# Transposing the softmax of the landmark queries on VectorE and moving it by DMA, in a fused Nystrom attention and feed-forward kernel

## The chip, the cores and the metric

The kernel runs on one core of a Trainium2 chip. A core has a matrix engine (TensorE, PE in the profile; its weight loads have a row of their own, PEld), a vector engine (VectorE, DVE), a scalar engine (ScalarE, ACT), a general engine (GpSimd, POOL) and a queue engine that here only issues DMAs (SyncE, SP). DMAs are also issued from POOL's and ACT's queues. The engines run side by side, each through its own list of instructions in order, and wait for one another by semaphores.

The metric is the device time of one execution, in microseconds. Three runs of the kernel before took 279.04, 278.62 and 277.09 us; the median is 278.62.

## What is computed

The reference, cut to its core: Nystrom attention over 8 batches, 8 heads, 576 tokens of 64 features, with 32 landmarks, each the mean of 18 tokens, and behind it a multiplicative feed-forward layer.

```python
q_lm = q.reshape(B, H, 32, 18, D).mean(axis=3)      # landmarks
k_lm = k.reshape(B, H, 32, 18, D).mean(axis=3)
A  = softmax(scale * q    @ k_lm^T)                 # 576 x 32
Bm = softmax(scale * q_lm @ k_lm^T)                 # 32 x 32
C  = softmax(scale * q_lm @ k^T)                    # 32 x 576
Z  = Bm^T / (norm1(Bm) * norminf(Bm) + 1e-6)
for _ in range(6):
    Z = 2 * Z - Z @ Bm @ Z
x = A @ Z @ C @ v                                   # 4608 x 512 over all heads
out = ((x @ w1) * (x @ w2)) @ w3 @ w_out            # 4608 x 512
```

## The kernel before, in words

**Units of work.** A quad is four heads of one batch: 16 quads, n = 0 to 15, two to a batch b. With 32 landmarks a head, the landmarks of a quad fill the 128 partitions. w3 @ w_out is computed once at the start (tasks `w3n`, `wf`, `wt`, `mm`), so that each batch's dense part needs two products alone: d (x by w1 and w2, 192 tokens at a time) with the product of both on VectorE (f), and g (by w3 w_out, 128 tokens at a time), copied out by ScalarE (h) and stored on SP's queue (`st`).

**One quad.** Q and K are loaded from POOL's queue (`lq`), transposed on VectorE (`tk`, `tq`), summed to landmarks on POOL (`ma`, `mb`, lines 529 and 536), or for the first two quads on TensorE. `S{n}` multiplies the landmark queries by K into the PSUM tile `wide` (`psS`), of which there is one. VectorE takes the rows' maximum (`sm`, lines 585 and 586), copies the 32 columns of B's scores out (`bo`, line 593), ScalarE takes the exponential (`se`, line 599) into `ec`, the E of the title, 128 landmarks (four heads by 32) by 576 tokens. To multiply E by V, tokens must lie on partitions: TensorE transposes E back into `wide` in four pieces of 128 columns and one of 64 (task `T{n}`, lines 607 and 609), and ScalarE copies that to `ecT` (`cm` and `cr`, lines 614 and 619). Only then is `wide` free for the next quad's scores. `C{b}` multiplies E by V (tiles `vb`, loaded on SP's queue, line 504), in 80 small matmuls of 32 columns of weights for both quads. The A side (`A`, `am`, `as`, `ae`, `au`, `an`, `tA`, `aT`) goes by beside it.

**Groups.** The inverse is iterated for two batches together (`ba` to `Z`), on TensorE in 32x32 tiles, and joined to C by `W`; `U{b}` multiplies the result by w1 and w2, and the batch's dense part follows.

**What sets the order.** Class `Plan` holds a list scheduler that runs while the kernel is built. Each task has an engine, a duration, what it needs, which buffers it takes and gives back, and a priority; the planner runs through time with a model of the engines and of the DMA queues and writes one order, and each engine's instructions are issued in it. `T0` and `PER` (65 and 20) set when a batch's dense part is due, `att`, `lane` and `cvt` the due times of quads, groups and of C. On TensorE a task's mode (full array, or tiles of 128x32, 64x32, 32x32, 128x64) has a bonus if it is the last task's (`MP`, `MT`, `MY`), so that modes stay together. An engine never overtakes its own list: who waits holds up all that is behind.

The lines that matter for the change:

```python
    def c_trans(n):                                     # line 603
        ...
            for c in range(4):
                nc.tensor.transpose(out=psS[:, 0, 128 * c:128 * c + 128], in_=ec[:, 128 * c:128 * c + 128],
                                    identity=ident[:, :])
            nc.tensor.transpose(out=psS[0:64, 1, 128:256], in_=ec[:, 512:S], identity=ident[:, :])
...
    def cv_mm(b):                                       # line 770
        ...
                        mm(ps[r, 64 * qd:64 * qd + 64], ecTs[at(f"ecT{n}")][:, c, r],
                           vbs[at(f"vb{n}")][:, h, c, :], start=(c == 0), stop=(c == 4), pos=(0, 32 * h))
```

Of the kernel before, what the change touches and what calls it, by code (L numbers as in the profile page):

```python
# [15 lines left out]
S = 576  # L16
# [9 lines left out]
MT = 7.0  # L26
MY = 2.0
# [18 lines left out]
class Plan:  # L46
# [6 lines left out]
    SLACK = 0.05  # L53

# [40 lines left out]
    def _transfers(self, limit):  # L95


        while True:
# [3 lines left out]
            if act:  # L102
                all_ = sum(h[2].share for h in act)
                stop = min(stop, self.clock + min(h[1] * all_ / h[2].share for h in act))
                for h in act:
                    h[1] -= max(0.0, stop - self.clock) * h[2].share / all_
# [8 lines left out]
    def run(self):  # L115
# [4 lines left out]
        def ended(t, end):  # L120
# [8 lines left out]
            for u in after.get(t.name, ()):  # L129
                waiting[u.name] -= 1  # L130
                if not waiting[u.name]:
                    u.ready = max(self.by[d].end for d in u.deps)
                    avail[u.eng].append(u)
# [14 lines left out]
        while len(order) < n:  # L148
# [41 lines left out]
            if t.move:  # L190
                self.queues[e].append([at + (dur + 0.75 if e == "POOL" else min(dur, 0.45)), t.move, t])
            else:
                ended(t, at + dur + t.lat)
# [5 lines left out]
def kernel(  # L199
# [41 lines left out]
    P.ring("vb", NV)  # L241
    ecs = slots(fixed, 2, [128, S], FP32, "ec")
    ecTall = fixed.tile([128, 4, 5, 128], FP32, name="ecT")
# [41 lines left out]
    T0 = 65.0  # L285
# [5 lines left out]
    def att(n):  # L291
        bs = GROUPS[GOF[n // 2][0]]
        k = n - 2 * bs[0] - 2 * len(bs) + 4
        first = dense(bs[0]) - 55.0 + 7.5 * k
        return max(12.0 + 6.0 * n, first)
# [7 lines left out]

    NE = int(2.0)
# [23 lines left out]
    def const_e():  # L328
        nc.gpsimd.memset(vball[64:128, :, :, 4, :], 0.0)
        nc.gpsimd.memset(ecTall[64:128, :, 4, :], 0.0)  # L330
        nc.gpsimd.memset(lmTall.rearrange("p i a l e -> p (i a l e)").bitcast(FP32), 0.0)

# [10 lines left out]
    add("ce", "POOL", 2.4, const_e, deps=["cb"], prio=-4.0)  # L343
# [59 lines left out]

    def w3_hi(j, h, c0, c1):
        def fn():
            nc.scalar.activation(out=w3t[at(f"w3t{j}")][:, 0, 128 * c0:128 * c1], in_=w3_src(j, h, c0, c1),  # L406
# [3 lines left out]
    def w3_lo(j, h, c0, c1):  # L410
        def fn():
            c, t = slice(128 * c0, 128 * c1), w3t[at(f"w3t{j}")]
            nc.vector.scalar_tensor_tensor(out=t[:, 1, c], in0=w3_src(j, h, c0, c1), scalar=WSC,  # L413
                                           in1=t[:, 0, c], op0=ALU.mult, op1=ALU.subtract)
        return fn

    def w34_mm(j, c, part=None):
        def fn():
            ps = bank(at(f"pw{j}"))
            t = w3t[at(f"w3t{j}")]  # L420
            cc = slice(128 * c, 128 * c + 128)
            if part != 1:
                mm(ps, t[:, 0, cc], wo[:, 0, c, :], start=(c == 0), stop=False)
            if part != 0:
                mm(ps, t[:, 0, cc], wo[:, 1, c, :], start=False, stop=False)
                mm(ps, t[:, 1, cc], wo[:, 0, c, :], start=False, stop=(c == 7))
# [8 lines left out]
    W1 = 0.0  # L435
    JS = int(3.0)
    JH = 0.0
# [4 lines left out]
    def w34_tasks():  # L442
        for j in range(8):
            p0 = 4.0 + 7.7 * j
            add(f"w3n{j}", "SP", 0.43 if j < PEB else 1.7, load_w3(j), acq=[("w3n", f"w3n{j}", 1, 3 if j == 0 and PEB else 2)],
                prio=-0.01 if j == 0 else 0.1 + 0.01 * W1 - 0.005 if j == 1 else p0 - 10.0,
                after=0.0 if j < 2 else max(0.0, p0 - 10.0 - 4.0), move=1.42 if j < PEB else 1.8,
                lat=1.7, share=3.8 if j < PEB else 2.5)
            if j == 0:
                for c in range(8):  # L450
                    if c % 2 == 0:
                        add(f"wf{c}", "SP", 1.72, load_wout(c), prio=0.1 + 0.01 * c, move=1.55, lat=1.7, share=2.1)
# [9 lines left out]
            for h, (c0, c1) in enumerate(cuts):  # L462
# [7 lines left out]
                    acq=[] if h else [("w3t", f"w3t{j}", 1, 8)], rel=[f"ptr{j}{h}"], prio=p0 - 3.5 + h)  # L470
# [3 lines left out]
            for c in range(8):  # L474
                hi, lo = [f"woh{c}", f"wh{j}{part[c]}"], [f"wol{c}", f"wl{j}{part[c]}"]
                bank1 = [("P", f"pw{j}", 1, 1)] if c == 0 else []
                if j < JS:
# [3 lines left out]
                        rel=[f"w3t{j}"], prio=p0 + 0.7 * c, mode="full")  # L481
                    continue
                add(f"mm{j}{c}", "PE", 0.65, w34_mm(j, c), deps=hi + lo + ([f"mm{j}{c - 1}"] if c else []),
                    acq=bank1, rel=[f"w3t{j}"], prio=p0 + 0.7 * c, mode="full")
# [12 lines left out]
    def load_v(n):  # L497
        def fn():
            b, qd = divmod(n, 2)
            vb = vbs[at(f"vb{n}")]  # L500
# [81 lines left out]
    def s_max(n):  # L582
        def fn():
            mx = tinies[at(f"mx{n}")]
            nc.vector.reduce_max(out=mx[:, 0:1], in_=s_cols(), axis=AX.X)
            nc.vector.tensor_scalar(out=mx[:, 1:2], in0=mx[:, 0:1], scalar1=-SCALE, scalar2=None, op0=ALU.mult)  # L586
        return fn

    def b_out(n):
        def fn():  # L590
            b, qd = divmod(n, 2)
            g, i = GOF[b]
            nc.vector.tensor_copy(out=bscs[at(f"bsc{g}")][:, 2 * i + qd, :], in_=psS[:, 1, 64:96])
        return fn

    def s_exp(n):
        def fn():
            b, qd = divmod(n, 2)
            nc.scalar.activation(out=ecs[at(f"ec{n}")], in_=s_cols(), func=AXF.Exp,  # L599
                                 scale=SCALE, bias=tinies[at(f"mx{n}")][:, 1:2], accum_out=tinies[at(f"tc{b}")][:, 2 + qd:3 + qd])  # L600
# [11 lines left out]
    def c_main(n):  # L612
        def fn():
            nc.scalar.copy(out=ecTs[at(f"ecT{n}")][:, 0:4, :].rearrange("p c x -> p (c x)"), in_=psS[:, 0, :])
        return fn

    def c_rest(n):
        def fn():
            nc.scalar.copy(out=ecTs[at(f"ecT{n}")][0:64, 4, :], in_=psS[0:64, 1, 128:256])
# [87 lines left out]
    def quad_tasks(n):  # L707
# [4 lines left out]
            after=max(L0, p - (20.0 if n < 4 else 20.0)), move=3.3, lat=0.9, share=4.6)  # L712
        add(f"lv{n}", "SP", 1.72, load_v(n), acq=[("vb", f"vb{n}", 1, 1)], deps=["ce"] if n < 4 else [], prio=cvt(b) - 8.0 + qd, after=max(12.0, cvt(b) - 8.0 - 3.0 + 3 * qd), move=1.95, lat=1.8, share=1.1)
# [10 lines left out]
        else:  # L724
# [11 lines left out]
            acq=[("S", f"S{n}", 1, 3)], rel=[f"Tk{n}", f"lmT{n}"], prio=p, mode="full")  # L736
# [8 lines left out]
        add(f"sm{n}", "DVE", 0.83, s_max(n), deps=[f"S{n}"], acq=[("tiny", f"mx{n}", 1, 1)], prio=p)  # L745
        new = n == 2 * GROUPS[GOF[b][0]][0]
        add(f"bo{n}", "DVE", 0.1, b_out(n), deps=[f"S{n}"] + ([] if new else [f"bo{n - 1}"]),
# [440 lines left out]
```

## Time and profile before

| | |
|---|---|
| median of three runs | 278.62 us (277.09 to 279.04) |
| profiled execution, its own time | 278.43 us |
| its span, first to last instruction | 276.6 us |
| granted TensorE clock | 0.995 |
| busy PE / DVE / ACT / POOL | 259.1 / 185.2 / 194.7 / 121.5 us |
| DMA packets | 26732, 37.32 MB, mean 135 GB/s |

The span is 1.8 us shorter than the execution's time. The page cuts the span into 40 slices of 6.9 us, with the busy tenths of each engine in each:

```profile
PE   3997799989989999999999999999999999999992
DVE  2659989979649995975887957776764562542530
ACT  3666858357469789867997698599858647758741
POOL 9435787996958884918866811003010000000000
DMA  7999999999763552895937671112111121122123
```

In the first nine slices the loads fill the DMA engines (240 to 259 GB/s in the page's row of bytes). From the thirteenth slice on TensorE is busy 90% or more in all slices but the last. DVE, ACT and POOL do the attention side until about the thirtieth slice and then only feed the dense part. A group of lines gives busy time, the mean of one instruction, and the idle time ahead of it with what ended it. A matmul's own duration holds its way through the array, so its pace is read from starts that follow each other, not from its mean.

### The profile page before, as it was taken

Reading aid. Unit: us, or ns where it says so; the run is one execution under the profiler, and the core shown is the slowest. Engines: PE = TensorE matmul, PEld = TensorE weight load, DVE = VectorE, ACT = ScalarE, POOL = GpSimd, SP = SyncE. Lnnn points to the kernel's source line nnn. Section 1 sums busy time; section 2 is a strip of 40 time slices with the busy share of each in tenths; the row PEclk is TensorE's granted clock in tenths of the full one; section 3 lists DMA queues with packets and bytes.
Section 4 is the critical chain, followed back from the end, with each engine's and each line's share of the span. In section 5 each row is a group of like instructions: output and inputs, shape, how many; then the busy total and the mean of one; then the engine's idle time right before and its main releaser. Section 6 shows DMA issues by size and latency. Waiting matters only on the chain.

```text
span 276.6 us, 9700 instructions
## 1 busy us (share of the span) xinstructions
PE 259.1 (94%) x3908; PEld 171.4 (62%) x3908; DVE 185.2 (67%) x526; ACT 194.7 (70%) x551; POOL 121.5 (44%) x145
## 2 busy tenths in 40 slices
PE   3997799989989999999999999999999999999992
PEld 3663464645447776766578667766875765765761
DVE  2659989979649995975887957776764562542530
ACT  3666858357469789867997698599858647758741
POOL 9435787996958884918866811003010000000000
PEclk9999999999999999999999999999999999999998
DMA  7999999999763552895937671112111121122123
GB/s 245 252 254 255 259 243 256 240 252 216 128 105 69 89 97 100 227 220 121 180 79 192 168 207 40 38 47 72 41 40 40 57 61 59 58 78 76 40 77 115
DMA packets 26732, 37.32 MB, mean 135 GB/s; under 512 B 3264, under 2 KB 16832, under 8 KB 26688
## 3 DMA queue, kind: packets, MB, share of 16 engines
q1 hardware_dynamic: 19664, 24.91, 30.4%
q0 software_dynamic: 6784, 11.54, 24.4%
q8 instruction: 30, 0.49, 0.7%
q10 hardware_dynamic: 240, 0.26, 0.3%
q14 instruction: 14, 0.11, 0.1%
HBM read 38.80 MB, written 9.44 MB: 174 GB/s over the span
## 4 chain that ended last, share of the span: by engine, by line
PE 59%; DMA 16%; POOL 14%; DVE 4%; ACT 3%; issue 2%; SPq 0%; POOLq 0%; ACTq 0%
PE bank L276 53%; POOL ls L536 6%; DMA nat<-in_q_dram 6%; POOL ls L529 5%; DMA u<-in_moe_w_out_dram 4%; PE wide L276 3%; DMA nat<-in_k_dram 3%; DMA ecT<-in_moe_w_out_dram 2%; POOL ah L681 2%; DMA osb<-in_moe_w_dram 2%; PE wide L607 1%; DVE wo L371 1%; POOL nat L492 1%; PE bank L690 1%; ACT asb L1020 1%
## 5 line engine op out<-in xcount | busy, mean ns | idle before, releaser
L276 PEld LDWEIGHTS <-u 128*128 128x128 f16 x960 | 80.4, 98 | 32.5 <-issue 6.4
L1026 DVE TENSOR_TENSOR ab<-asb,bank 128x192 f16<-128x192 f16 x192 | 59.2, 346 | 43.2 <-ACT asb L1020 42.8
L276 PE MATMUL bank<-aT,u 128*128 128x192 f16 x768 | 77.0, 246 | 0.0
L276 PE MATMUL bank<-w,ab 128*128 128x512 f16 (+1 forms) x296 | 73.4, 374 | 0.0
L1020 ACT CAST asb<-bank 128x192 f16<-128x192 f32 x192 | 56.5, 333 | 22.3 <-PE bank L276 20.3
L276 PE MATMUL bank<-wo,u 128*128 128x512 f16 x192 | 47.8, 379 | 2.7 <-DVE wo L371 1.5
L529 POOL TENSOR_TENSOR ls<-nat 128x1152 f32<-128x1152 f16 x14 | 33.2, 2373 | 26.9 <-DMA nat<-in_q_dram 12.0
L536 POOL TENSOR_TENSOR ls<-ls 128x128 f32<-128x128 f32 (+2 forms) x56 | 40.7, 727 | 3.8
L276 PEld LDWEIGHTS <-ab 128*128 128x128 f16 x296 | 26.9, 98 | 20.8 <-issue 2.9
L681 POOL TENSOR_TENSOR ah<-ea,tiny 128x512 f16<-128x512 f32 (+1 forms) x16 | 18.5, 1159 | 44.0 <-DVE tiny L675 35.8
L938 ACT CAST u<-bank 128x512 f16<-128x512 f32 x64 | 34.4, 605 | 3.4 <-PE bank L276 3.4
L1052 ACT ACTIVATE osb<-bank 128x512 f32<-128x512 f32 x35 | 21.2, 605 | 8.8 <-PE bank L276 8.8
L566 ACT COPY lmT<-lmu 32x128 f16<-32x128 f16 x64 | 18.8, 294 | 4.6 <-DVE lmu L557 3.7
L276 PE MATMUL bank<-w,wT 64*32 64x512 f16 x512 | 18.9, 380 | 0.3 <-ACT u L938 0.2
L276 PEld LDWEIGHTS bank<-xz 32*32 32x32 f32 x768 | 11.2, 105 | 8.4 <-issue 2.1
L276 PE MATMUL bank<-xz 32*32 32x64 f32 (+1 forms) x768 | 14.8, 213 | 0.3 <-DVE xz L884 0.3
L599 ACT ACTIVATE ec<-wide,tiny 128x576 f32<-128x576 f32 x16 | 12.0, 749 | 4.4 <-DVE tiny L586 3.6
L413 DVE SCALAR_TENSOR_TENSOR u<-bank,u 128x512 f16<-128x512 f32 (+2 forms) x17 | 10.9, 638 | 5.6 <-ACT u L406 5.6
L276 PEld LDWEIGHTS <-Tq 128*128 128x128 f16 x160 | 10.6, 97 | 5.3 <-issue 1.9
L406 ACT ACTIVATE u<-bank 128x512 f16<-128x512 f32 (+2 forms) x17 | 9.7, 571 | 5.3 <-PE bank L276 4.5
L521 DVE STREAM_TRANSPOSE Tk<-nat 128x448 f32<-128x448 f32 (+1 forms) x32 | 13.1, 447 | 0.0
L674 DVE TENSOR_REDUCE tiny<-ea 128x16 f32<-128x512 f32 (+1 forms) x16 | 11.7, 732 | 1.4 <-ACT ea L668 1.4
(95 smaller groups left out, 322.5 us busy)
## 6 DMA issues: line engine op xcount, KB each, us to landing
vb<-in_v_dram SPq DMA_DIRECT2D x32, 160.0 KB, 4.3
out_dram<-osb SPq DMA_DIRECT2D x37, 128.0 KB, 2.3
nat<-in_k_dram POOLq DMA_DIRECT2D x16, 288.0 KB, 6.0
nat<-in_q_dram POOLq DMA_DIRECT2D x16, 288.0 KB, 7.8
vb<-in_v_dram SPq DMA_DIRECT2D x32, 128.0 KB, 4.4
out_dram<-osb SPq DMA_DIRECT2D x16, 256.0 KB, 2.4
w3n<-in_moe_w_dram SPq DMA_DIRECT2D x16, 128.0 KB, 7.7
w<-in_moe_w_dram POOLq DMA_DIRECT2D x8, 256.0 KB, 10.3
```

The costliest lines, as they stand in the source:

```text
L276: nc.tensor.matmul(out_, lhsT, rhs, start=start, stop=stop, **({} if pos is None else {"tile_position": pos}))
L521: nc.vector.transpose(out=T[:, to:to + r1 - r0].rearrange("p r l e -> p (r l e)").bitcast(FP32), in_=nats[at(f"nat{n}")][:, t, r0:r1].rear ...
L529: nc.gpsimd.tensor_tensor(out=l, in0=nat[:, :, 0:9, :], in1=nat[:, :, 9:18, :], op=ALU.add)
L536: nc.gpsimd.tensor_tensor(out=l[:, :, x:x + m, :], in0=l[:, :, x:x + m, :], in1=l[:, :, y:y + m, :], op=ALU.add)
L566: nc.scalar.copy(out=lm[r, :, h, :], in_=u[r].rearrange("p t l e -> p t (l e)"))
L599: nc.scalar.activation(out=ecs[at(f"ec{n}")], in_=s_cols(), func=AXF.Exp, scale=SCALE, bias=tinies[at(f"mx{n}")][:, 1:2], accum_out=tinies ...
L674: nc.vector.reduce_sum(out=t[:, 20:20 + g], in_=eas[at(f"ea{n}")][:, 0:g, :], axis=AX.X)
L681: nc.gpsimd.tensor_tensor(out=ahs[at(f"ah{n}")][:, 0:g, :], in0=eas[at(f"ea{n}")][:, 0:g, :], in1=tinies[at(f"ta{n}")][:, 0:g].unsqueeze(2 ...
L938: nc.scalar.copy(out=uu[at(f"u{b}{qd}")][:, wi, 512 * half:512 * half + 512], in_=bank(at(f"pU{b}{wi}{half}{qd}")))
L1020: nc.scalar.copy(out=asb[at(f"as{b}{j}{th}")], in_=bank(at(f"pD{b}{j}{th}"))[:, 0:THIRD])
L1026: nc.vector.tensor_mul(ab[:, j, c0:c0 + THIRD], asb[at(f"as{b}{j}{th}")], bank(at(f"pD{b}{j}{th}"))[:, THIRD:2 * THIRD])
L1052: nc.scalar.activation(out=osb[at(f"os{t}")], in_=bank(at(f"pE{t}")), func=AXF.Copy, scale=2.0 ** -12)
```

## The change

For quads 6 to 15 (batches 3 to 7; `NT` is 6) E isn't transposed on TensorE. VectorE transposes it in 32x32 blocks into `ecx` (`e_trans`, task `et`): afterwards tokens lie on partitions, but each block still stands on the 32 partitions of its head. 16 DMAs a batch on SP's queue (`e_move`, tasks `lx{b}{x}`, four to a task, one for each head) then move each block row from the 32 partitions of head h to the 32 partitions of token group x in `ecT`, for both quads at once, in runs of 640 or 512 bytes. `ecx` is their source, one buffer for a batch; `ecT` is laid out with the head ahead of the column group in all quads. `wide` is given back after the exponential and the copy of B's scores. The five transposes and both copies of these quads go.

For all quads the copy of B's scores (`bo`) and the factor on the maximum move from VectorE to ScalarE. The memset of `ecT` becomes a task of its own, behind the w_out work (`cz`). V's buffers are named by n modulo 4. The product of w3's fourth block is split into a high and a low part as the first three were (`JS` 4), the high part's priority moves forward (`JH` 3), the second w3 load goes behind the first w_out load (`W1`). Planner constants change: `T0` 65 to 64, `MT` 7 to 6, `MY` 2 to 2.5, latencies and shares of the loads, the due times of the w1/w2 loads, and a margin (`ROOM`) for tasks that are due early.

The diff's core:

```diff
-MT = 7.0
-MY = 2.0
+MT = 6.0
+MY = 2.5
...
-    ecTall = fixed.tile([128, 4, 5, 128], FP32, name="ecT")
+    ecTall = fixed.tile([128, 4, 4, 5, 32], FP32, name="ecT")
+    ecx = fixed.tile([128, 2, 4, 5, 32], FP32, name="ecx")
+    P.ring("ecx", 1)
...
-    T0 = 65.0
+    T0 = 64.0
...
+    NT = 2 * int(3.0)
...
-        nc.gpsimd.memset(ecTall[64:128, :, 4, :], 0.0)
...
+    def const_f():
+        nc.gpsimd.memset(ecTall[64:128, :, :, 4, :], 0.0)
...
+    add("cz", "POOL", 0.5, const_f, deps=[f"wol{c}" for c in range(4)], prio=1.5)
...
-    W1 = 0.0
-    JS = int(3.0)
-    JH = 0.0
+    W1 = 1.0
+    JS = int(4.0)
+    JH = 3.0
...
-            nc.vector.tensor_scalar(out=mx[:, 1:2], in0=mx[:, 0:1], scalar1=-SCALE, scalar2=None, op0=ALU.mult)
...
-            nc.vector.tensor_copy(out=bscs[at(f"bsc{g}")][:, 2 * i + qd, :], in_=psS[:, 1, 64:96])
+            nc.scalar.copy(out=bscs[at(f"bsc{g}")][:, 2 * i + qd, :], in_=psS[:, 1, 64:96])
...
+            nc.scalar.activation(out=mx[:, 1:2], in_=mx[:, 0:1], func=AXF.Copy, scale=-SCALE)
...
+    def e_trans(n):
+
+        def fn():
+            x, ec = ecx[:, n % 2], ecs[at(f"ec{n}")]
+            nc.vector.transpose(out=x[:, :, 0:4].rearrange("p x c l -> p c x l"),
+                                in_=ec[:, 0:512].rearrange("p (c x t) -> p c x t", c=4, x=4))
+            nc.vector.transpose(out=x[:, 0:2, 4], in_=ec[:, 512:S].rearrange("p (x t) -> p x t", x=2))
+        return fn
+
+    def e_move(b, x):
+        def fn():
+            i = P.slot[f"ecT{2 * b}"][0]
+            w = 5 if x < 2 else 4
+            for h in range(4):
+                nc.sync.dma_start(
+                    out=ecTall[32 * x:32 * x + 32, i:i + 2, h, 0:w, :].rearrange("p q c l -> p q (c l)"),
+                    in_=ecx[32 * h:32 * h + 32, :, x, 0:w, :].rearrange("p q c l -> p q (c l)"))
         return fn
...
-                add(f"lw{s}{qd}{wi}", "POOL", 0.62, load_w12(s, qd, wi), prio=T0 - 12.0 + 3.0 * s + wi,
-                    after=T0 - 12.0 - 4.0 + 3.0 * s, move=1.5, lat=0.9, share=2.1)
+                add(f"lw{s}{qd}{wi}", "POOL", 0.62, load_w12(s, qd, wi), prio=T0 - 10.0 + 5.0 * s + wi,
+                    after=T0 - 10.0 - 4.0 + 5.0 * s, move=1.4, lat=1.83, share=5.3)
...
-            acq=[("S", f"S{n}", 1, 3)], rel=[f"Tk{n}", f"lmT{n}"], prio=p, mode="full")
+            acq=[("S", f"S{n}", 1, 2 if n >= NT else 3)], rel=[f"Tk{n}", f"lmT{n}"], prio=p, mode="full")
...
-        add(f"T{n}", "PE", 0.54, c_trans(n), deps=[f"se{n}", "cb"], rel=[f"ec{n}"], prio=p + 2.0, mode="full")
-        add(f"cm{n}", "ACT", 0.5, c_main(n), deps=[f"T{n}"], acq=[("ecT", f"ecT{n}", 1, 1)], rel=[f"S{n}"],
-            prio=p + 2.5)
-        add(f"cr{n}", "ACT", 0.18, c_rest(n), deps=[f"T{n}", f"cm{n}"], rel=[f"S{n}"], prio=p + 2.5)
+        if n >= NT:
+            add(f"et{n}", "DVE", 0.8, e_trans(n), deps=[f"se{n}"], acq=[] if qd else [("ecx", f"ecx{b}", 1, 4)],
+                rel=[f"ec{n}"], prio=p + 2.0)
+            for x in range(4 * qd):
+                add(f"lx{b}{x}", "SP", 1.72, e_move(b, x), deps=[f"et{n - 1}", f"et{n}", "cz"],
+                    acq=[] if x else [("ecT", f"ecT{n - 1}", 2, 1)], rel=[f"ecx{b}"], prio=p + 3.0 + 0.1 * x,
+                    move=0.45, lat=1.9, share=0.8)
+        else:
+          add(f"T{n}", "PE", 0.54, c_trans(n), deps=[f"se{n}", "cb"], rel=[f"ec{n}"], prio=p + 2.0, mode="full")
+          add(f"cm{n}", "ACT", 0.5, c_main(n), deps=[f"T{n}", "cz"], acq=[("ecT", f"ecT{n}", 1, 1)], rel=[f"S{n}"],
+              prio=p + 2.5)
+          add(f"cr{n}", "ACT", 0.18, c_rest(n), deps=[f"T{n}", f"cm{n}"], rel=[f"S{n}"], prio=p + 2.5)
```

## The prediction

> **What bounds the kernel now.** I read the shares of the engines first, then the busy time by stage, then the timeline of TensorE, then the waits.
>
> ```profile
> PE 259.1 (94%) x3908; PEld 171.4 (62%) x3908; DVE 185.2 (67%) x526; ACT 194.7 (70%) x551; POOL 121.5 (44%) x145
> ```
> ```profile
> 20.00:78.00 58.00, 52.51 (x681) 28.39 (x680) 50.13 (x121) 35.02 (x92) 46.55 (x52) 1.00 1.02 223
> 78.00:100.00 22.00, 20.36 (x370) 15.46 (x369) 18.88 (x51) 18.95 (x60) 16.88 (x20) 1.00 0.48 84
> 100.00:207.00 107.00, 106.53 (x1794) 74.19 (x1792) 78.96 (x241) 85.35 (x257) 46.21 (x47) 1.00 0.48 121
> 207.00:271.40 64.40, 64.33 (x867) 42.64 (x864) 27.75 (x89) 43.52 (x122) 0.00 (x0) 1.00 0.19 63
> ```
> Columns of the stages: from and to, length, then busy PE, PE's weight loads, DVE, ACT, POOL (instructions in brackets), granted clock, DMA share, GB/s. From 100 us to the end of the matmuls PE rests 0.5 us in 171. Is busy also dense? In the timeline of the last stage, four and sixteen matmuls follow each other without a hole:
>
> ```profile
> 255.06 1.81 PE L276 MATMUL bank<-aT,u 128*128 128x192 f16 x20
> 256.70 1.03 PE L276 MATMUL bank<-w,ab 128*128 128x512 f16 x4
> ```
> Twenty matmuls of 192 columns take 256.70 - 255.06 = 1.64 us, 82 ns each, and this pace is the same wherever no wait is printed. So work taken off PE after 78 us comes off the span, until another engine is late.
>
> **A. The transposes of E on PE (line 607, 609), taken from quads 6 to 15.**
>
> ```profile
> 88.59 0.61 PE L607 MATMUL wide<-ident,ec 128*128 128x128 f32 x4
> 89.03 0.27 PE L609 MATMUL wide<-ident,ec 128*64 128x128 f32 x1
> 89.14 1.81 PE L276 MATMUL bank<-aT,u 128*128 128x192 f16 x20
> ```
> From 88.59 to the start of the next work at 89.14 is 0.55 us a quad; ten quads give **-5.5 us**. All ten stand after 88 us, in the dense stages.
>
> A rule of the Trainium skill speaks against this part: VectorE: DVE Perf Modes, sections "The three transpose paths" and "Rules for kernel authors", sends a 128x128 transpose to TensorE where its result may go to PSUM, and gives 390 ns there against 311 ns on VectorE, which turns 32x32 blocks alone. With its 390 ns for each of five transposes, an estimate, part A would be -19.5 us; the row's 0.55 us for five pipelined ones decides, and the sum goes by it.
>
> **B. What comes with it on ACT and DVE.**
>
> ```profile
> L614 ACT COPY ecT<-wide 128x512 f32<-128x512 f32 x16 | 9.7, 606 | 0.7 <-PE wide L609 0.6
> L619 ACT COPY ecT<-wide 64x128 f32<-64x128 f32 x16 | 4.3, 270 | 0.0
> L400 DVE STREAM_TRANSPOSE bank<-w3n 128x512 f32<-128x512 f32 x8 | 5.6, 705 | 0.0
> L521 DVE STREAM_TRANSPOSE Tq<-nat 128x64 f32<-128x64 f32 x8 | 1.6, 202 | 0.0
> L586 DVE TENSOR_SCALAR tiny<-tiny 128x1 f32<-128x1 f32 x16 | 2.5, 154 | 0.6
> L593 DVE COPY bsc<-wide 128x32 f32<-128x32 f32 x16 | 3.0, 187 | 3.8 <-ACT ec L599 3.6
> ```
> ACT loses 10 x (0.606 + 0.270) = 8.8 us of copies. It takes over two small operations of all 16 quads, the factor of the maximum and the copy of B's scores; the nearest ACT rows are 203 ns (128x1, behind the exponential) and 270 ns (64x128), so 16 x 0.47 = 7.5 at most: net -1.3 us. DVE gains ten pairs of block transposes, 10 x (0.705 + 0.202) = 9.1, the strided row of line 400 being the nearest form, and loses 16 x (0.154 + 0.187) = 5.5: net +3.6 us. Over 100 to 207 us DVE goes from 79 to about 79 + 8 x 0.91 - 8 x 0.34 = 83.5 of some 102 us (82%), ACT stays near 81%. PE's work hides both there: 0 us. Between 78 and 100 us DVE goes from 18.9 to 20.0 of 21 us and has no cover left; a loss of up to 1.1 us or, through the copies that ACT drops, a gain of as much. I take 0, both ends kept.
>
> The scores' tile (`wide`) is now given back after the exponential, not after both copies. PE's waits show what that is worth:
>
> ```profile
> PE wide L276 <- ACT ecT L619: 2.0, 3, 1.0
> ```
> Of the three only the one at 97.07 us (0.63) belongs to a quad from 6 on; the 1.0 at 80.03 is quad 5's. **-0.6 us**.
>
> **C. The way of E to its partitions: 16 DMAs a batch on SP's queue.** No SBUF-to-SBUF DMA is in the trace, so bounds are taken from the queue's other DMAs, lines 504 (V, 32 partitions each, as here) and 1067 (stores):
>
> ```profile
> L504 SPq DMA_DIRECT2D vb<-in_v_dram x64: 311/430/1677, 26.9 to 160.3; - x64
> DMA to landing us min/median/max: 2.7/4.3/8.8
> ```
> ```profile
> L1067 SPq DMA_DIRECT2D out_dram<-osb x55: 538/549/1716, 99.0 to 272.1; - x55
> ...
> DMA to landing us min/median/max: 1.9/2.4/8.4
> ```
> In the instruction order each DMA of SP waits for the one eight places ahead, so with landings of 4.3 us the pace can't be under 4.3/8 = 0.54 us. From the first issue to the last landing: low end 16 x 0.31 + 1.9 = 6.9 us; middle 16 x 0.43 + 2.4 = 9.3; with landings in HBM-load traffic 16 x 0.43 + 4.3 = 11.2; high end 16 x 0.54 + 4.3 = 12.9.
>
> What covers it? The matmuls of E with V (task C) wait for the last of these, and PE goes in order: all dense work behind C waits too. The changed order puts, between S15 and C7 on PE, six half output tiles (0.87 each by the timeline), 18 groups of four 192-column matmuls (0.33), C6 (1.27), and transposes, scores and others (2.5): 14.9 us. Ahead of the DMAs DVE needs 5.3 us of it (maximum 0.69, pair 0.91, sum and reciprocal 0.94, four products 1.10, B's start 0.58, pair 0.91, and some 0.2 to start). Cover: about **9.5 us**. The other batches stand alike. So low end and middle are hidden; 11.2 costs 1.7, 12.9 costs 3.4 a batch. From the middle I take none for four batches and 1.7 for batch 4, whose DMAs fall into 110 to 120 us with its V and Q/K loads in flight (214 GB/s): **+1.7 us**, ends 0 and 5 x 3.4 = 17.
>
> Two things are queued behind: stores of the output on SP, up to 9 us late, with four buffers for tiles that come every 4.5 us (18 us of cover: 0); and on DVE the first transpose of a batch, which waits until the single buffer of the batch ahead has been sent. Between the pairs of batches 6 and 7 DVE has only some 7.5 us of other work, under the middle's 9.3; but the products that it holds up have PSUM banks ahead of them. In the ends above.
>
> **D. The order.** Weights of the planner change (a mode's hold on PE 7 to 6, and others). Counted in the instruction order, PE leaves its full mode 57 times, not 53: C4 and C5, C6 and C7 no longer run in pairs. Price: a pair takes 2.40 us (197.52 to 199.92), one alone 1.27 (85.05 to 86.32), so 0.14 to change back, and 0.09 to enter by the stretch before: 4 x 0.23 = **+0.9 us**.
>
> Ahead of 78 us the chain of waits runs on POOL (sums for the means) and loads:
>
> ```profile
> 62.81 0.61 POOL L511 DMA_DIRECT2D w<-in_moe_w_dram x1 [0.76 <-DMA w<-in_moe_w_dram]
> 65.02 0.61 POOL L511 DMA_DIRECT2D w<-in_moe_w_dram x1 [1.59 <-DMA nat<-in_k_dram]
> 65.64 2.38 POOL L529 TENSOR_TENSOR ls<-nat 128x1152 f32<-128x1152 f16 x1
> ```
> Quad 6's sum stood behind eight loads of w1/w2, which had to wait for landings; now behind four. It can start up to some 5 us earlier. PE rests 58 - 52.5 = 5.5 us between 20 and 78, of which 1.4 (8.56 of 10 busy) in 70 to 80, behind that chain. I take **-1.4 us**, the rest that lies there; ends -5.5 and +2 (the second half of w1/w2 lands later, 10.3 us after its issue by the row, against its use at 81.5 us). The earlier start of one w_out load, the split of one more weight product and the extra memset move 0.1 to 0.5 us of work into those rests: 0.
>
> **Sum.** -5.5 - 0.6 + 1.7 + 0.9 - 1.4 = -4.9 us. The profiled execution took 278.43 us (span 276.6, 1.8 around it), 0.2 under the median of the three runs (278.62): 278.4 - 4.9 = **273.5 us**.
>
> **Rivals.**
> 1. The eviction side becomes the bound, nothing is gained: about 278 us. For it: DVE is 86% busy in 78 to 100 and 94% in 90 to 100 already and gets 3.6 us more; between 80 and 160 each of PE's holes that is closed must be fed by an ACT copy and a DVE product. Against: 82% from 100 to 207. Chance 0.15. A rule of the skill leads to the same time: Perfetto Trace Analysis, section "Identifying the Most-Contended Engine", judges TensorE by its weight loads, not by busy matmuls; by their 62% PE would have room and lose nothing by the transposes. The trace disagrees where it can be tested: in 207 to 271 weight loads are 66% busy while 192 columns go through every 82 ns.
> 2. **Slower:** the DMAs outlast their cover at every C. At 12.9 us a batch PE stands 5 x 3.4 = 17 us: 278.4 - 6.6 + 17 = 288.8 us. It turns to a loss from 6.6/5 = 1.3 us beyond the cover, 10.8 us from first issue to last landing. For it: V's landings (4.3). Against: those read HBM in the load phase; batches 6 and 7 move theirs when DMA is below 20%, and 40 KB are a quarter of a V load. Chance 0.15.
> 3. More is won: all rests between 20 and 78 us go as well: 278.4 - 6.6 - 4.1 = 267.7, against it the loads, at 223 GB/s over that stage. Chance 0.12.
> That the transposes stay on PE can be left out: the instruction order has 20 block transposes of E on DVE, 80 DMAs, and 50 fewer matmuls.
>
> **How the numbers follow.** Forecast: 0.58, by itself 271 to 276. Range: down to 269.0, which cuts off about half of rival 3, and up to 279.5, which holds rival 1 and leaves out most of rival 2. A measurement of this kernel tells about 1% (2.8 us) from no change: below 275.8 is faster. Faster: 0.12 and nearly all of the forecast's 0.58, 0.69; same: rival 1 and what is left, 0.16; slower: 0.15.
>
> **What would show it.** A right: the groups of lines 607/609's counterpart count 24 and 6 matmuls, and the time from the first dense matmul to the end falls by about 5 us. B: DVE below 90% in 100 to 200, and waits of PE for the ACT copies of E gone from quad 7 on. C: SBUF DMAs landing 2 to 3 us after issue at 0.3 to 0.45 us apart; wrong if PE's waits list the moved E with over 3 us in total. D: quad 6's sum starting near 60 us; PE's rest in 70 to 80 under 0.5. The forecast fails above all if the moves land late, or if rests between 78 and 160 grow by what the transposes free.

## The result and the profile after

| | before | after |
|---|---|---|
| median | 278.83 us (4 runs, 277.09 to 279.15) | 299.03 us (4 runs, 298.41 to 299.47) |
| profiled execution, its own time | 278.43 us | 298.63 us |
| span | 276.6 us | 296.9 us |
| granted TensorE clock | 0.995 | 0.968 |
| PE busy / not busy in the span | 259.1 / 17.5 us | 263.3 / 33.6 us |

The changed kernel takes 1.0737 times as long (95% interval 1.0686 to 1.0788). The forecast was 273.5 us, the range 269.0 to 279.5. In the ratios here and below, executions well above a kernel's fastest are left out; the one of twobuf that was profiled is such a one (373.89 us at a granted clock of 0.66), so its trace isn't read.

**The page of the kernel after**, busy time, TensorE's slices and its granted clock, and the chain that ended last:

```profile
PE 263.3 (89%) x3858; PEld 171.5 (58%) x3858; DVE 189.5 (64%) x514; ACT 196.1 (66%) x563; POOL 122.9 (41%) x145
...
PE   3797999899998399999579799994998999999993
...
PEclk9999999999999979999959999998699999999998
...
PE 60%; DMA 18%; SPq 11%; DVE 4%; ACT 3%; issue 2%; POOL 1%; DVEq 0%; ACTq 0%; POOLq 0%
```

Before, TensorE's row was at 9 from the thirteenth slice on. Now it has holes at slices 14, 20, 21, 23 and 28 (7.4 us each), and in or right behind 14, 20 and 28 the granted clock is down as well. SP's queue, an engine that computes nothing, holds 11% of the chain. The **waits of TensorE and of VectorE** (total, times, longest, in us; each from the list of its engine) name the causes:

```profile
PE bank L285 <- DVE ab L1080: 9.6, 4, 5.1
PE bank L285 <- DMA out_dram<-osb: 5.5, 1, 5.5
...
PE bank L285 <- DMA ecT<-ecx: 2.6, 6, 0.8
```
```profile
DVE ecx L651 <- DMA out_dram<-osb: 5.4, 1, 5.4
DVE ecx L651 <- DMA ecT<-ecx: 4.9, 1, 4.9
```

Only 2.6 us stand under the moved E (`ecT<-ecx`) by name. The 5.5 us under `out_dram<-osb` are the same wait: what waited is the product of E with V, which needs no store; the first store left the queue right behind the last move, and the name printed is that of this neighbour. The 9.6 us under DVE are the same cause once removed: VectorE's block transposes (line 651) stood 5.4 and 4.9 us for moves of the batch ahead to land, and TensorE stood behind the products of the dense part (line 1080) that VectorE had queued after them. The **timeline of TensorE** has these three rests:

```profile
97.88 1.03 PE L285 MATMUL bank<-w,ab 128*128 128x512 f16 x4
104.43 2.77 PE L285 MATMUL bank<-vb,ecT 128*32 128x64 f32 x80 [5.52 <-DMA out_dram<-osb]
...
150.22 0.80 PE L285 MATMUL bank<-aT,u 128*128 128x192 f16 x4 [5.08 <-DVE ab L1080]
...
207.56 0.80 PE L285 MATMUL bank<-aT,u 128*128 128x192 f16 x4 [3.93 <-DVE ab L1080]
```

C5 (165.7 to 168.6 us) and C7 (222.1 to 225.0) stood another 1.8 and 1.0 us, in pieces. That makes 17.3 us of rests that the moves end; TensorE's time without work grew by 16.1 (33.6 - 17.5).

Why the moves are late is in the **queue of SP**. First the line of the moves (duration of the issue, minimum/median/maximum in ns), then the queue's timeline for batch 3:

```profile
L661 SPq DMA_DIRECT2D ecT<-ecx x80: 585/596/1856, 90.1 to 221.9; - x80
...
DMA to landing us min/median/max: 1.8/2.0/6.2
```
```profile
90.13 11.50 SPq L661 DMA_DIRECT2D ecT<-ecx  x16
101.73 0.65 SPq L1121 DMA_DIRECT2D out_dram<-osb  x1
```

A single move occupies the queue for 0.596 us in the median, the next starts some 0.64 us after it or later, and 16 of them take 11.5 us before the last is even issued. From the first issue to the last landing the five batches need 14.7, 16.6, 13.7, 12.8 and 14.2 us.

The remaining loss isn't a wait. The **stretches of the span** around the first rest (from, to, length, busy PE, weight loads, DVE, ACT, POOL, granted clock, DMA share, GB/s):

```profile
102.00:104.00 2.00, 0.00 (x0) 0.00 (x0) 0.00 (x0) 0.00 (x0) 1.84 (x3) 0.98 0.99 252
...
105.00:106.00 1.00, 1.00 (x46) 1.00 (x45) 0.00 (x0) 0.00 (x0) 0.00 (x0) 0.50 0.00 0
...
108.00:109.00 1.00, 1.00 (x9) 0.34 (x6) 0.00 (x0) 0.76 (x3) 0.00 (x0) 1.00 0.00 0
```

When the work comes back, the clock is granted at 0.50. It stands there from 103.9 to 107.3 us, and around the ends of the other two rests from 148.3 to 155.1 and from 206.3 to 213.1. The product that starts at 104.43 takes 2.77 us; in the kernel before 80 such matmuls take 1.34:

```profile
97.62 1.34 PE L276 MATMUL bank<-vb,ecT 128*32 128x64 f32 x80
```

Half of the time at half clock in which TensorE had work is lost work: about 1.45 + 2.44 + 2.79 = 6.7 us.

### The profile page after: what moved, and what is told of

Read it like the earlier page. It is cut to its first block, busy times and chain, and to the rows that moved or that the text cites. A ratio compares the mean times of both kernels' runs of the same rounds, so it can differ in the third digit from the quotient of the medians.

```text
span 296.9 us, 9664 instructions
## 1 busy us (share of the span) xinstructions
PE 263.3 (89%) x3858; PEld 171.5 (58%) x3858; DVE 189.5 (64%) x514; ACT 196.1 (66%) x563; POOL 122.9 (41%) x145
## 4 chain that ended last, share of the span: by engine, by line
PE 60%; DMA 18%; SPq 11%; DVE 4%; ACT 3%; issue 2%; POOL 1%; DVEq 0%; ACTq 0%; POOLq 0%
PE bank L285 56%; SPq L661 9%; DMA vb<-in_v_dram 4%; DMA ecT<-ecx 4%; DMA nat<-in_q_dram 4%; PE wide L285 3%; DMA out_dram<-osb 2%; DMA w3n<-in_moe_w_dram 2%; DMA osb<-in_moe_w_dram 1%; DVE ecx L651 1%; SPq L1121 1%; PE bank L734 1%; SPq L528 1%; DVE wo L386 1%; ACT ec L624 1%
## 5 line engine op out<-in xcount | busy, mean ns | idle before, releaser
L285 PEld LDWEIGHTS <-u 128*128 128x128 f16 x960 | 81.4, 99 | 46.2 <-issue 16.5
L285 PE MATMUL bank<-aT,u 128*128 128x192 f16 x768 | 79.7, 250 | 9.9 <-DVE ab L1080 9.6
L1074 ACT CAST asb<-bank 128x192 f16<-128x192 f32 x192 | 57.2, 329 | 30.7 <-PE bank L285 29.2
L285 PE MATMUL bank<-w,ab 128*128 128x512 f16 (+1 forms) x296 | 75.1, 381 | 0.0
L725 POOL TENSOR_TENSOR ah<-ea,tiny 128x512 f16<-128x512 f32 (+1 forms) x16 | 18.9, 1187 | 55.8 <-ACT u L991 16.9
L285 PEld LDWEIGHTS <-ab 128*128 128x128 f16 x296 | 27.5, 99 | 22.5 <-issue 5.1
L1106 ACT ACTIVATE osb<-bank 128x512 f32<-128x512 f32 x35 | 21.1, 603 | 10.9 <-PE bank L285 10.2
L285 PE MATMUL bank<-vb,ecT 128*32 128x64 f32 x640 | 14.1, 232 | 8.5 <-DMA out_dram<-osb 5.5
L285 PEld LDWEIGHTS bank<-vb,ecT 128*32 128x32 f32 x640 | 12.0, 117 | 11.3 <-issue 9.0
L285 PEld LDWEIGHTS bank<-xz 32*32 32x32 f32 x768 | 11.3, 105 | 7.3 <-issue 2.1
L437 DVE SCALAR_TENSOR_TENSOR u<-bank,u 128x512 f16<-128x512 f32 (+2 forms) x17 | 10.8, 642 | 6.2 <-ACT u L431 6.1
L651 DVE STREAM_TRANSPOSE ecx<-ec 128x512 f32<-128x512 f32 x10 | 7.1, 708 | 11.3 <-DMA out_dram<-osb 5.4
L845 ACT ACTIVATE cv<-bank,tiny 128x64 f32<-128x64 f32 x16 | 4.2, 314 | 15.0 <-PE bank L285 13.2
```

The costliest lines, as they stand in the source:

```text
L285: nc.tensor.matmul(out_, lhsT, rhs, start=start, stop=stop, **({} if pos is None else {"tile_position": pos}))
L437: nc.vector.scalar_tensor_tensor(out=w3t(j, 1, c0, c1), in0=w3_src(j, h, c0, c1), scalar=WSC, in1=w3t(j, 0, c0, c1), op0=ALU.mult, op1=ALU ...
L651: nc.vector.transpose(out=x[:, :, 0:4].rearrange("p x c l -> p c x l"), in_=ec[:, 0:512].rearrange("p (c x t) -> p c x t", c=4, x=4))
L725: nc.gpsimd.tensor_tensor(out=ahs[at(f"ah{n}")][:, 0:g, :], in0=eas[at(f"ea{n}")][:, 0:g, :], in1=tinies[at(f"ta{n}")][:, 0:g].unsqueeze(2 ...
L1074: nc.scalar.copy(out=asb[at(f"as{b}{j}{th}")], in_=bank(at(f"pD{b}{j}{th}"))[:, 0:THIRD])
L1106: nc.scalar.activation(out=osb[at(f"os{t}")], in_=bank(at(f"pE{t}")), func=AXF.Copy, scale=2.0 ** -12)
```

## The experiments

In the ratios each kernel is set against the kernel before, run on the same chip beside it. Where an edit touches what the planner is told (nt16, late, p2x, p3b, p2x4), the planner writes a new order, and the comparison holds that too.

**nomove: the order, without the moves.** Is it the transfer, or something else in the new order?

```diff
-                nc.sync.dma_start(
-                    out=ecTall[32 * x:32 * x + 32, i:i + 2, h, 0:w, :].rearrange("p q c l -> p q (c l)"),
-                    in_=ecx[32 * h:32 * h + 32, :, x, 0:w, :].rearrange("p q c l -> p q (c l)"))
+                pass
```

> The 80 moves are left out, so the product of E with V in batches 3 to 7 reads what lay in its buffer before; instruction order, block transposes on DVE and all else as changed. Queue theory (16 issues at 0.64 us and the landings, 12.8 to 16.6 us a batch, outlast what covers them, and TensorE's clock falls in the waits): no waits for E are left, 273 us (270 to 276), granted clock above 0.99. Rival one (the block transposes make VectorE the bound) and rival two (the other edits of the order cost the time): 290 us or more, with the same rests.

Measured: 273.29 us, 0.9801 (0.9753 to 0.9850); span 271.7, granted clock 1.00. So everything that the change loses hangs on the 80 DMAs: 296.9 - 271.7 = 25.2 us of span. Against this kernel, with the same instructions in the same order, the changed one has 33.6 - 16.7 = 16.9 us more rest and 263.3 - 255.0 = 8.3 us more busy time, of which the half clock explains some 6.7; the other 1.6 are not broken down. That 273.29 comes within 0.2 us of the forecast is chance: the forecast has 1.7 us for moves in it, and its other terms add up to 271.8.

The page of this kernel, and its stretch from 100 to 207 us:

```profile
PE 255.0 (94%) x3858; PEld 166.3 (61%) x3858; DVE 189.4 (70%) x514; ACT 195.3 (72%) x563; POOL 122.9 (45%) x145
```
```profile
100.00:207.00 107.00, 106.13 (x1923) 72.64 (x1912) 82.52 (x245) 86.67 (x264) 44.57 (x46) 1.00 0.48 121
```

DVE is 77% busy there (82.52 of 107) and TensorE 99%: the eviction side isn't the bound (rival 1 falls).

**nt16: the new order with all transposes on TensorE.** This separates part D from A and B.

```diff
-    NT = 2 * int(3.0)
+    NT = 2 * int(8.0)
```

> NT 16 in place of 6: E of all quads is transposed on TensorE again; every other edit of the change stays. Queue theory and rival one: 278 us (275 to 281), since only 10 transposes of 0.55 us come back to a kernel of 273. Rival two: 290 us or more.

Measured: 277.65 us, 0.9961 (0.9925 to 0.9998). The order and the planner's constants are worth -1.3 us, with an interval that ends just below no change. From here to nomove, where the transposes and copies are gone, are 277.65 - 273.29 = 4.4 us.

**late: the same moves, and a planner that is told what they take.** The planner had been given 1.72 us for four moves and 1.9 us to land.

```diff
-                add(f"lx{b}{x}", "SP", 1.72, e_move(b, x), deps=[f"et{n - 1}", f"et{n}", "cz"],
+                add(f"lx{b}{x}", "SP", 2.56, e_move(b, x), deps=[f"et{n - 1}", f"et{n}", "cz"],
...
-                    move=0.45, lat=1.9, share=0.8)
+                    move=0.45, lat=3.7, share=0.8)
```

> The planner is told the measured cost of the moves: four issues take 2.56 us in place of 1.72, and they have landed 4.6 us after their start in place of 2.8. The same work in another order. Queue theory: most of the waits go, 281 us (275 to 288); what is left are batches 3 and 4, whose landings are slowed by loads in flight. Rivals one and two: no better than 293.

Measured: 280.75 us, 1.0072 (1.0036 to 1.0107). Two constants of the planner bring back 18.3 of the 25.7 us between the changed kernel and nomove, and the moves are no faster: first issue to last landing is 14.4, 15.2, 15.8, 12.7 and 13.8 us, 71.9 in all, against 72.0 before the edit. What changed is what stands between them and the product. TensorE's timeline and waits:

```profile
105.38 2.33 PE L285 MATMUL bank<-vb,ecT 128*32 128x64 f32 x80 [1.44 <-DMA out_dram<-osb]
```
```profile
PE bank L285 <- DMA out_dram<-osb: 1.4, 1, 1.4
PE bank L285 <- DMA ecT<-ecx: 1.2, 4, 0.4
```

In the changed kernel TensorE reached C3 98.9 - 90.1 = 8.8 us after the first move was issued; here it does 105.38 - 1.44 - 91.18 = 12.8 us after, with more groups of the dense part, a weight product and the scores of a quad put ahead. The rest at C3 falls from 5.52 to 1.44 us, and at the block transposes no wait for moves is left. So the moves' length alone doesn't make the loss; the loss hangs on the difference between it and the cover that the order gave them. This kernel is still 7.5 us above nomove: its waits for moves come to 2.6 us in the list above, and TensorE is busy 258.6 us against 255.0; the rest isn't broken down.

**issue: what one DMA holds its queue for.** A kernel of DMAs alone, 16 of each form (8 and 4 of those with 64 and 128 partitions), in its core:

```python
    nc.sync.dma_start(out=a2[o, h], in_=src[i, :, x, 0:160])     # L69: as the moves
    nc.sync.dma_start(out=a1[o, h], in_=src[i, 0, x, :])         # L73: one run of 1280 B
    # L77: four runs of 320 B;  L81, L83: 64 and 128 partitions;  L87: from HBM, runs as in L69
    # L91: from SBUF to HBM;  L96, L100: L69 from ACT's and from POOL's queue
```

> No attention and no dense part, only DMAs on queues: sixteen times the move's form (32 partitions, 2 runs of 640 B), then one run of 1280 B, 4 runs of 320 B, 64 partitions, 128 partitions, a load from HBM and a store to it of the move's form, and the move's form on ACT's and POOL's queues. If the issue is priced by the run, one run takes some 0.35 us and 4 runs, 64 and 128 partitions 1 us or more; if by the DMA, all take about 0.6; if by where the data come from and go to, loads take 0.43, stores 0.55, moves 0.6.

Measured, by the line of this kernel (ns, minimum/median/maximum):

```profile
L69 SPq DMA_DIRECT2D moved<-src x16: 586/610/789, 11.6 to 22.1; - x16
L73 SPq DMA_DIRECT2D moved<-src x16: 588/589/675, 22.7 to 32.3; - x16
L77 SPq DMA_DIRECT2D moved<-src x16: 588/589/596, 33.0 to 42.5; - x16
L83 SPq DMA_DIRECT2D moved<-src x4: 611/621/623, 48.4 to 50.4; - x4
L87 SPq DMA_DIRECT2D loaded<-in_moe_w_dram x16: 390/426/428, 0.7 to 7.8; - x16
L91 SPq DMA_DIRECT2D out_dram<-src x16: 587/593/650, 51.5 to 61.1; - x16
L96 ACTq DMA_DIRECT2D movedact<-src x16: 592/607/649, 11.6 to 21.9; - x16
L100 POOL DMA_DIRECT2D movedpool<-src x16: 536/536/668, 11.8 to 19.9; - x16
```

One, two or four runs and 32 or 128 partitions cost the same, 0.59 to 0.62 us. What counts is where the source lies: 0.43 us from HBM with the same destination, 0.59 from SBUF, to SBUF or to HBM. The row that comes nearest to a move is thus the store's, not that of V's loads. Landing is no matter of form either: 1.9 us alone (L73), 2.6 for L69, which ran beside two other queues.

**twoq: half of the moves on POOL's queue**, same order.

```diff
-                nc.sync.dma_start(
+                (nc.sync if x < 2 else nc.gpsimd).dma_start(
```

> The changed kernel and its order, but the moves of token groups 2 and 3 are issued on POOL's queue at the same place. If the issue time of one queue is what outlasts the cover: 8 x 0.64 = 5.1 us on SP beside 8 x 0.54 = 4.3 on POOL, and landings of 2 to 4 us, 7 to 9 us a batch under the cover of 9.5: 276 us (273 to 281), granted clock above 0.99. If it is the landings (the same 80 transfers, the same loads beside them): 290 or more. POOL waits for DVE's transposes at these places, which may hold up its sums in batch 3.

Measured: 286.8 us, 1.0289 (1.0254 to 1.0324), outside of what was expected. Half of the loss is gone and the moves take 11.9, 9.6, 14.3, 8.2 and 10.7 us. Batch 5 stays as long (14.3, and 13.7 in the changed kernel) because POOL also computes. Its timeline:

```profile
148.72 2.38 POOL L553 TENSOR_TENSOR ls<-nat 128x1152 f32<-128x1152 f16 x1 [4.13 <-ACT lm L567]
151.18 3.15 POOL L560 TENSOR_TENSOR ls<-ls 128x512 f32<-128x512 f32 x4
154.45 4.32 POOL L661 DMA_DIRECT2D ecT<-ecx  x8
```

SP's half of the batch began at 147.5 us; POOL's stood behind a wait of 4.13 us and two sums of 5.5 us that the planner, which had all moves on SP, had put there. C5 rested 3.46 us. The expectation had halved the issue time and forgotten what is queued ahead on the second engine.

**twobuf: two `ecx` buffers by turns**, on SP's queue as in the changed kernel. If the block transposes' wait for the single buffer is a cause of its own, it goes.

```diff
-    ecx = fixed.tile([128, 2, 4, 5, 32], FP32, name="ecx")
+    ecxs = [fixed.tile([128, 2, 4, 5, 32], FP32, name=f"ecx{i}") for i in range(2)]
...
-            x, ec = ecx[:, n % 2], ecs[at(f"ec{n}")]
+            x, ec = ecxs[n // 2 % 2][:, n % 2], ecs[at(f"ec{n}")]
```

> The changed kernel and its order, but two buffers for the block transposes, by turns. Only DVE's two waits for the moves of the batch ahead go (5.4 and 4.9 us, behind which PE rested 5.1 and 3.9); the product's own waits stay, and what DVE no longer delays meets the same queue: 290 us (286 to 294). If the single buffer is the whole cause: 280 or less.

Measured: 297.13 us, 1.0642 (1.0598 to 1.0686), outside of what was expected: some 2 us off the changed kernel, not 9. So the single buffer is where the wait stands, but a second one wins little. Why it wins no more isn't shown. Sharing one queue doesn't explain it by itself: in the changed kernel SP's queue was free 6.3 us ahead of batch 5's first move (147.33 to 153.64 us), though only 1.4 us ahead of batch 7's (208.23 to 209.59).

**p2x: two queues and a planner that knows it.** twoq's split, with durations and latencies of each queue (SP 2.56 and 4.7 us, POOL 2.15 and 3.5).

```diff
-                add(f"lx{b}{x}", "SP", 1.72, e_move(b, x), deps=[f"et{n - 1}", f"et{n}", "cz"],
-                    acq=[] if x else [("ecT", f"ecT{n - 1}", 2, 1)], rel=[f"ecx{b}"], prio=p + 3.0 + 0.1 * x,
-                    move=0.45, lat=1.9, share=0.8)
+                sp = x < 2
+                add(f"lx{b}{x}", "SP" if sp else "POOL", 2.56 if sp else 2.15, e_move(b, x),
+                    deps=[f"et{n - 1}", f"et{n}", "cz"],
+                    acq=[], rel=[f"ecx{b}"], prio=p + 3.0 + 0.1 * x,
+                    move=0.45, lat=4.7 if sp else 3.5, share=0.8)
```

(`ecT` is now taken by the second quad's block transpose.)

> Two queues as in twoq, and the planner is told of it: four issues 2.56 us on SP, 2.15 on POOL, all landed 5.6 us after the first of four. Queue theory: 274 us (271 to 277), under both the kernel before and the run without moves plus 1.5; rival (landings): 280 or more.

Measured: 276.36 us, 0.9925 (0.9885 to 0.9965), in the range expected, but some 3 us above nomove, where 1.5 had been allowed for. The moves take 10.7, 7.7, 9.0, 11.0 and 8.8 us; the longest rest at a product is 0.96 us, at C3.

**p3b: p2x with two `ecx` buffers and `T0` 63.**

> As p2x, with two buffers for the block transposes and T0 63 in place of 64. Queue theory: 274 us (270 to 277); if the buffer matters once the queue is halved, 1 to 2 us under p2x, else the same within 1 us.

Measured: 278.14 us, 0.9974 (0.9935 to 1.0013), missed. Neither helped. The two ratios' intervals overlap, so it isn't shown that this kernel is slower than p2x, and as both edits went together they can't be told apart.

**warm: the changed kernel, with TensorE kept busy in the first rest.** Does the half clock come from the rest? 20 products of 512 columns whose result is overwritten go ahead of C3:

```diff
             ps = bank(at(f"pC{b}"))
+            for _ in range(20 if b == 3 else 0):
+                mm(ps, ident16[:, :], w34[:, 0, :])
```

> The changed kernel with 20 matmuls of 512 columns more, ahead of batch 3's product of E with V, into that product's own bank, which the product then overwrites: 4.3 us of work in a place where TensorE rested 5.5 us. In the changed kernel the granted clock stood at 0.50 from there for some 3 us. If the half clock comes from the rest: it stays at 1.00 through that product, 1 to 2 us off the changed kernel's time, 297.5 (296 to 299). If it comes from anything else there: still 0.50, and the time the same or longer, 299 to 303.

Measured: 300.53 us, 1.0840 (1.0774 to 1.0905). The mechanism is there; the time isn't. TensorE's timeline, and a stretch right behind the rest that has 46 matmuls in the changed kernel:

```profile
98.47 4.48 PE L285 MATMUL bank<-w,ident 128*128 128x512 f16 x20
104.24 1.72 PE L285 MATMUL bank<-vb,ecT 128*32 128x64 f32 x80 [1.29 <-DMA out_dram<-osb]
```
```profile
105.00:106.00 1.00, 1.00 (x74) 0.91 (x70) 0.00 (x0) 0.00 (x0) 0.00 (x0) 1.00 0.07 16
```

The clock stays at 1.00, the product takes 1.72 us, not 2.77, and the next work of 192 columns starts at 108.34, not 109.64 us: 1.3 us won at this place. The later rests (5.46 us up to 149.0 us, 1.57 up to 164.5, 3.18 up to 206.9, 1.35 up to 221.8) and the clock take it back: TensorE resumes work 1.2 us ahead of the changed kernel at 149.00 and 0.7 ahead at 206.91, and the span ends 1.3 us later. Behind the second and the fourth of these rests, at C5 and C7, the granted clock is now at 0.50 from 165.8 to 169.2 and from 223.8 to 227.2 us, where the changed kernel has 1.00. Together the four stretches at half clock lose 1.56 + 1.53 + 1.62 + 1.71 = 6.4 us of work, against 6.7 in the changed kernel: the half clock went from one place to others. The intervals of the two ratios overlap (1.0774 to 1.0788), so that the whole is slower than the changed kernel isn't shown, only that it isn't faster by the 1 to 2 us expected.

**p2x4: p2x with one batch fewer on the new way** (`NT` 8: batch 3, whose moves leave beside loads, keeps its transposes on TensorE).

```diff
-    NT = 2 * int(3.0)
+    NT = 2 * int(4.0)
```

> As p2x (two queues, planner told), with NT 8 in place of 6: batch 3 keeps its transposes on TensorE. In p2x batch 3's moves, beside loads in flight, still took 10.7 us and its product 3.4 us in place of 1.1. Queue theory: 3.2 us of rest go, 1.1 us of transposes come back, 274.5 us (273 to 276.5); if the rest there was not due to the moves: 277.5.

Measured: 274.95 us (11 runs), 0.9887 (0.9853 to 0.9922), as expected: 1.1% below the kernel before, below the changed one, and 2.7 us below nt16, which has the new order alone. So the change pays once its moves have two queues and the planner knows what they take. Its moves take 7.3, 10.0, 6.3 and 9.1 us. The page, and the wait for moved E in the list of TensorE's waits:

```profile
PE 258.9 (94%) x3868; PEld 168.3 (61%) x3868; DVE 188.2 (69%) x510; ACT 195.7 (71%) x567; POOL 139.9 (51%) x177
```
```profile
PE bank L285 <- DMA ecT<-ecx: 0.2, 1, 0.2
```

## Why the prediction was wrong

| part | predicted | measured |
|---|---|---|
| A and B, transposes and copies | -5.5 - 0.6 = -6.1 us | -4.4 (nt16 to nomove) |
| C, the moves | +1.7 (0 to 17) | +25.7 (nomove 273.29 to changed 299.03) |
| D, the order | +0.9 - 1.4 = -0.5 | -1.3 (before 278.97 to nt16) |
| sum | -4.9 | +20.0 (the two medians differ by 20.2) |

**A and B were right in kind, and 1.7 us too high.** 24 and 6 transposes are left, in place of 64 and 16. DVE is at 77% from 100 to 207 us in nomove, below the 82% worked out. Most of the 1.7 us are rests of TensorE that the freed work left open: from 78 to 100 us it rests 0.84 us in nomove and none in nt16, and from 100 us to its end 0.87 against 0.26. The first is the stage in which the prediction saw no cover left for DVE and took 0.

**D came near in number, and in part by luck.** The forecast's -0.5 lies within the interval of -1.3 (-2.1 to -0.1). Both of its signs came: TensorE has no rest in 70 to 80 us in the changed kernel, where it had 1.4, and quad 6's sum starts at 57.05 us, not 65.64 (the lines below). But this rest didn't leave the span. In the first 78 us TensorE rests 10.1 us in the kernel before and 10.2 in nt16, 10.3 in nomove; what is gained from 20 us on is lost ahead of it, where the order of the first products changed too. What nt16 has less is rest from 78 to 100 us, 0.00 against 1.64. No run measures the +0.9 for C in single batches.

```profile
70.00:80.00 10.00, 10.00 (x167) 5.61 (x164) 7.20 (x18) 6.66 (x20) 6.75 (x9) 1.00 0.91 153
```
```profile
57.05 2.45 POOL L553 TENSOR_TENSOR ls<-nat 128x1152 f32<-128x1152 f16 x1
```

**C is the step that failed**, by three terms:

1. *"middle 16 x 0.43 + 2.4 = 9.3", the nearest rows being "lines 504 (V, 32 partitions each, as here) and 1067 (stores)".* The issue was priced by V's loads since they have as many partitions. Partitions don't matter; the source does, and the store's row, from SBUF, stood beside it with 0.55 us. A move holds the queue for 0.60 us and the next comes at 0.64: 16 x 0.64 = 10.2 us of issue alone, more than the whole middle, and the sign named for C, moves 0.3 to 0.45 us apart, failed. With landings of 2 to 6 us, and stores between the moves, 12.8 to 16.6 us came out. The "high end" of 12.9, 16 x 0.54 + 4.3, was in truth about the low one, because its 0.54 had been worked out as a limit by landings and not taken from the queue's own pace.
2. *"Cover: about 9.5 us. The other batches stand alike."* The size was fair (8.8 us at C3, 11.3 at C5, 12.5 at C7 in the trace after), but the cover is a product of the planner's belief that 4 moves take 1.72 us and land in 1.9: it puts the product as close behind as that allows. The run late shows it: with the belief corrected, the same 72 us of moves cost 7.5 us more than none (280.75 - 273.29), not 25.7. The batches weren't alike either: at batches 4 and 6 the product came 25.0 and 23.8 us after the first move and the loss fell on the block transposes. There *"the products that it holds up have PSUM banks ahead of them"* failed: 5.08 and 3.93 us of TensorE's rest.
3. *The half clock was not in the sum.* It came to about 6.7 us, and follows from TensorE's rests, of which the forecast had none.

**Rival 2 was the case**, with a chance of 0.15 and a price of 288.8 us. Its turning point, 10.8 us from first issue to last landing, holds for the order that it was worked out from: 12.8 to 16.6 lie above it. It is no property of the moves alone, since late, with 12.7 to 15.8, is 1.8 us from the kernel before. Its price was too low by the same term: 72.0 - 5 x 9.5 = 24.5 in place of 17 gives 278.4 - 6.6 + 24.5 = 296.3 against the 298.6 of the profiled execution. That it comes so near is in part chance, since the rests are 17 us and the clock gives the other 7. What spoke against the rival, that batches 6 and 7 move their E when DMA is below 20% and that 40 KB are little, was about bandwidth; the limit is the number of DMAs on one queue. The sign that the prediction named, "wrong if PE's waits list the moved E with over 3 us in total", would have passed at 2.6 us by its letter: the waits stood under a store and under DVE.

**Rival 3** (267.7 us) had no part in it: even with no moves the time is 273.29, and rests of 16.7 us stay in the span.

The chances put 0.15 on slower. The spread between the middle and the high end of C was 5 x 3.4 us, more than all gains together, and the choice within it rested on a resemblance (32 partitions) that no row tested. The store's row would have given 16 x 0.55 + 2.4 = 11.2 us a batch, a loss of 5 x 1.7 = 8.5 and a time of some 280.3 us, outside of the range; that is still far from 299, since the queue's real pace, the block transposes' wait and the half clock are not in it.

## What to carry to other kernels

Price a group of small DMAs by its count times the queue's own time for one with the same kind of source, then add a landing, and hold that against the time from first issue to the consumer; bytes and DMA share say nothing about it. When a planner writes the order, its constants decide what a transfer costs: here the same 80 moves cost 25.7 us when they were announced too short and 7.5 when they were announced about as long as they are. Look for a late transfer also under other names, a store that follows it on the queue or an engine that waits for its source buffer.

## What the runs showed of the hardware

- A DMA's time on the issuing queue goes by its source: 0.59 to 0.62 us from SBUF, 0.43 from HBM on SP; 0.61 from SBUF on ACT's queue and 0.54 on POOL's. From 32 to 128 partitions and from one to four runs it is the same. The Trainium skill, DMA: Bandwidth & Descriptors, "Issuing engines are not separate DMA queues", says that issuing from several engines saves only the sequencer's time, "which is usually small relative to the DMA itself". Here the second half doesn't hold: 16 x 0.60 = 9.6 us of issue stand beside landings of 2.0, and splitting them over two queues took 12 us off the kernel.
- An SBUF-to-SBUF DMA of 32 or 40 KB landed 1.8 us after its issue at the best, 2.0 in the median, and up to 6.2 us when loads were in flight (batches 3 and 4; 252 GB/s at 102 to 104 us); in batches 5 to 7 it was 3.8 us at most. A kernel of DMAs alone gave 1.9 us (L73, one run).
- The granted clock of the changed kernel falls at 103.91, 148.28 and 206.31 us, the last two 13 and 30 times 3.413 us behind the first, and stands at 0.50 for 3.41, 6.83 and 6.83 us: it changes on a fixed beat of 3.41 us. As far as these traces tell, what counts is how busy TensorE was in one such beat, not how long a single rest was. From the changed kernel, warm and twoq in turn (columns as in the stretches above, busy PE first, clock third from the end):

```profile
202.89:206.31 3.42, 0.72 (x6) 0.34 (x4) 0.71 (x2) 2.36 (x10) 0.00 (x0) 1.00 0.31 94
206.31:209.72 3.41, 2.16 (x8) 1.16 (x8) 3.34 (x13) 0.58 (x2) 1.05 (x1) 0.50 0.51 171
209.72:213.13 3.41, 3.41 (x34) 2.10 (x33) 2.03 (x8) 1.08 (x3) 0.00 (x0) 0.50 0.20 48
```
```profile
162.36:165.78 3.42, 1.26 (x9) 0.47 (x7) 0.58 (x3) 1.02 (x3) 2.82 (x2) 1.00 0.22 56
165.78:169.19 3.41, 3.05 (x92) 2.25 (x90) 0.00 (x0) 0.52 (x2) 2.43 (x4) 0.50 0.81 227
```
```profile
100.66:104.08 3.42, 1.64 (x63) 1.25 (x67) 2.07 (x7) 2.26 (x9) 3.40 (x6) 1.00 0.14 38
104.08:107.49 3.41, 3.41 (x57) 1.68 (x46) 0.00 (x0) 1.46 (x5) 3.33 (x3) 0.50 0.87 151
```

  A beat with TensorE busy 1.64 us (twoq, where no single rest there was over 1.7 us) is followed by one at half clock; one with 1.68 (155.28 to 158.69 us in twoq) is not. From half clock the changed kernel came back after beats with 2.89 us of work and more, not after 1.47 or 2.16, so the first return took 2.9 us from the resumed work and the others 4.9 and 5.6. Other products in the first rest kept it at 1.00. The three times at half clock cost 1.5 to 2.8 us beyond the rests. The Trainium skill, TensorE: Matmul & The Clock Gate, "Part 1: The HAM clock gate", has half rate after an idle window of about 3.4 us and full rate after as long a busy one, by a window that runs freely. The trace agrees with the two levels, the length and the free run of the window; it differs in that the window need not be idle throughout: TensorE was busy in nearly half of it and the clock still fell.
